# Left-over expert code before the last window, an early scatter read from the gather buffer, and pools that wait as wholes

## The chip, the cores and the metric

The kernel runs on one NeuronCore of a Trainium2 chip. The metric is the device time of one execution in microseconds (us). The engines are named as in the profile: PE (TensorE, matmuls), DVE (VectorE), ACT (ScalarE), POOL (GpSimd), SP (SyncE, which here only issues DMAs). A name with a q behind it (PEq, POOLq) is that engine's sequencer: branches, semaphore waits, DMA issues.

## The reference, cut to what matters

Three layers run one after the other. The change lies in the third, a routed layer of eight experts; every token is served by one expert alone.

```python
x = attention(...)                       # 8 heads of 64, windowed, with global keys
x = _moe_ref(x, mu_k, mu_r, w_k, w_v, w_r)   # shift, relu^2 MLP, sigmoid gate: [4, 544, 512]

# _moe2_ref: for every token (2176 of them)
e = argmax(logits[b, s])  if s == 0 or local_gate[b, s] < 0.5  else prev_e
p = softmax(logits[b, s])
h = np.maximum(x[b, s] @ w1[e], 0.0)     # 512 -> 1024
out[b, s] = p[e] * (h @ w2[e])           # 1024 -> 512
```

## The kernel before, in words

**Phase 1** (0 to 541 us) computes attention, the second layer and the routing: for each expert a list of its tokens in chunks of 128 (`idx`), each token's weight (`acc`, read as `pcol`), and the number of chunks of each expert (`cint`, from it the largest, `cmax`). The second layer's result lies in device memory as `y`. **Phase 2** (541 to 791 us) is the expert layer. A *window* is up to two chunks of one expert: `full` computes two chunks, `tail` one. For a window POOL gathers the chunk's rows of `y` into `xs` (L859, an indirect DMA), PE transposes them (L866) into PSUM, ACT and DVE split the result into a high and a low part (`xh` L868, `xl` L869), and each product is three matmuls (L21 high by high, L23 weight low, L24 operand low). `pht` is the hidden layer; `hs`, `hh` and `hl` carry it on (L909, L897, L898); `po` is the second product; DVE scales it (`osb`, L924) and POOL scatters the rows to the output `out_dram` (L925, an indirect DMA).

Expert weights come from device memory in parts of 512 KB: SP fetches a part into a staging tile `st` or `sw` (L769), ACT splits off the high half (L778) and DVE or POOL the low half (L781), into one of four pairs of weight slots. Expert e uses slots 2 and 0 when e is even, 1 and 3 when it is odd, so the next expert's weights load while this one computes.

For this input the experts have 242, 127, 267, 483, 495, 321, 218 and 23 tokens, that is 2, 1, 3, 4, 4, 3, 2 and 1 chunks. The code is fixed for two windows of every expert (four chunks); further chunks are *left-overs*. The number of chunks is known at run time alone, so the windows stand under `If`s on registers (`first`, `more`). Expert 0's first chunk is computed ahead, still in phase 1, by `Experts.ahead`: its product ends in `poa`, DVE scales it into the phase-1 tile `oa` (L844), and POOL sends it off by the *early scatter* (L846), whose list of rows `idx` is a phase-1 tile too. Phase 2 therefore starts with `tail(0)`, the second chunk of expert 0. After the loop over experts 1 to 7 two blocks stand under `If`s: the left-overs of expert 0 (L972) and those of the others (L978). With these counts neither block is entered: all engines jump over both.

Memory: phase 1 and phase 2 use the same on-chip memory one after the other. Before the change the phase-2 pools say `reuse_waits="tile"`: each phase-2 tile waits for those phase-1 tiles that lay in its own place. The order of instructions on an engine is the order of the program here (phase 2 is scheduled by hand); a wait holds the engine's queue.

Of the kernel before, what the change touches and what calls it, by code (L numbers as in the profile page):

```python
# [12 lines left out]
PSUM=bass.MemoryType.PSUM; DRAM=bass.MemoryType.DRAM  # L13
# [319 lines left out]
class Mix:  # L333
# [360 lines left out]
    def finish(s,ps):  # L694

        nc=s.nc; t=s.const
        s.ci=t([P,E],"cint",I32); s.cm=t([P,1],"cmax",I32); cf=t([P,E],"cf")
        nc.vector.tensor_tensor(out=s.ci,in0=ps,in1=s.up,op=ALU.add)
        nc.vector.tensor_scalar(out=s.ci,in0=s.ci,scalar1=7,scalar2=None,op0=ALU.logical_shift_right)
        nc.vector.tensor_copy(cf,s.ci)  # L700
        nc.vector.tensor_reduce(out=s.cm,in_=cf,axis=X,op=ALU.max)
def phase1(tc,ctx,i,const,y,ident,x,slots,early,place,right):

# [47 lines left out]
class Experts:  # L751

    def __init__(s,tc,ident,w1,w2,y,out,slots):
        s.tc=tc; s.nc=tc.nc; s.ident=ident; s.w=(w1,w2); s.y=y; s.out=out
        s.w2done=False; s.slots=slots; s.loaded=0; s.staged=[]; s.K=2

        s.o=[1]+[0]*(E-1); s.m=[1]+[NCH]*(E-1)
    def slot(s,e,which): return s.slots[((2,0),(1,3))[e%2][which]]
    def views(s,e,which):

# [29 lines left out]
    def ahead(s,m):  # L790
# [49 lines left out]
        yield op("P",0.0,("cm",),(),lambda: s.w2done)  # L840
        ps=cm("poa")
        for f in range(8): yield from mm(ps,hh[:,f],hl[:,f],w2h[:,f],w2l[:,f],f==0,f==7)
        yield op("D",.61,("r",),("cm",))
        o=m.temp("oa"); nc.vector.tensor_scalar(out=o,in0=ps,scalar1=pc,scalar2=None,op0=ALU.mult)  # L844
        yield op("G",1.1,(),("r",))
        nc.gpsimd.indirect_dma_start(out=s.out,out_offset=IndirectOffsetOnAxis(ap=idx,axis=0),in_=o,in_offset=None,bounds_check=T-1,oob_is_err=False)  # L846
    def alloc(s):
        w=s.work

        new=[s.xwork.tile([P,1024],F32,name=f"sw{i}",bufs=1) for i in range(NST)]  # L850
        s.xs+=[s.xwork.tile([P,2,D],F32,name=f"xs{i}",bufs=1) for i in range(1,s.K)]
        s.x=[[s.xwork.tile([P,4,256],F32R,name=f"x{q}{i}",bufs=1) for q in "hl"] for i in range(3)]
        s.h=[w.tile([P,8,256],F32R,name=f"h{q}",bufs=1) for q in "hl"]
        s.st+=new; s.free+=new
    def gather(s,e,k):
        i=k%s.K
        for j in range(min(2,s.m[e]-2*k)):
            ch=e*NCH+s.o[e]+2*k+j
            s.nc.gpsimd.indirect_dma_start(out=s.xs[i][:,j,:],out_offset=None,in_=s.y,in_offset=IndirectOffsetOnAxis(ap=s.idx[:,ch:ch+1],axis=0))  # L859
    def prep(s,i,e,k,hf):  # L860

        nc=s.nc; xh,xl=s.x[i]; n=min(2,s.m[e]-2*k); N=n*P
        pt=s.ps.tile([P,2,256],F32,tag="pt",name="pt",bufs=2)
        for d in range(2):
            for j in range(n):
                nc.tensor.transpose(pt[:,d,j*P:(j+1)*P],s.xs[k%s.K][:,j,(2*hf+d)*P:(2*hf+d+1)*P],s.ident)  # L866
        sl=slice(2*hf,2*hf+2)
        nc.scalar.activation(xh[:,sl,:N],pt[:,:,:N],AF.Copy)  # L868
        nc.vector.tensor_sub(xl[:,sl,:N],pt[:,:,:N],xh[:,sl,:N].bitcast(F32))  # L869
# [77 lines left out]
    def run(s):  # L947
# [1 line left out]

        at=lambda e,k: (e%2,2)[k%2]  # L950
        s.gather(0,0)
        _,cs=s.nc.values_load_multi_w_load_instructions(s.counts[0:1,0:E],min_val=0,max_val=NCH); cmax=s.nc.values_load(s.cmax[0:1,0:1],min_val=0,max_val=NCH)
        s.cs=cs
        for _ in range(max(0,8-LN)):
            p=s.staged.pop(0); list(s.split(*p)); s.free.append(p[3])
# [4 lines left out]
        def others(e):  # L960
            if e+1>=E: return []
            def last():
                s.prep(at(e+1,0),e+1,0,1)
                if e+2<E: s.gather(e+2,0)
            return [lambda: (s.gather(e+1,1),s.prep(at(e+1,0),e+1,0,0)),last]

        s.tail(at(0,0),0,0,[s.whole]*min(8,16-LN),others(0))
        for e in range(1,E):
            s.first(at(e,0),at(e,1),e,cs[e],[s.whole]*8 if e+1<E else (),own(e),others(e))
        def weights(e):  # L970
            for q in range(8): list(s.split(*s.part(e,q,s.st[q%len(s.st)])))
        with tc.If(cs[0]>=2):  # L972
            s.o[0]=2; s.m[0]=NCH-2; weights(0)
            for k in range(NK-1):
                with tc.If(cs[0]>=2*k+2):
                    s.gather(0,k); s.prep(k%2,0,k,0); s.prep(k%2,0,k,1)
                    s.more(k%2,0,k,cs[0],1)
        with tc.If(cmax>=2*K+1):  # L978
            for e in range(1,E):
                with tc.If(cs[e]>=2*K+1):  # L980
                    weights(e)
                    for k in range(K,NK):
                        with tc.If(cs[e]>=2*k+1):
                            s.gather(e,k); s.prep(k%2,e,k,0); s.prep(k%2,e,k,1)
                            s.more(k%2,e,k,cs[e])

def program(tc,ins,out):
    nc=tc.nc
    with ExitStack() as ctx:
# [16 lines left out]
            m=phase1(tc,st,ins,const,y,ident,x,slots,early,place,right)  # L1006
            x.idx,x.pcol,x.counts,x.cmax=m.idx,m.acc[:,E*NCH:],m.ci,m.cm

        t=dict(reuse_waits="tile")
        x.xwork=p("xwork",**t); x.work=p("work",**t); x.ps=Pools("pt",p("pst",space=PSUM,**t),p("ps2",space=PSUM,**t))  # L1010
        x.alloc()
        slots.append(pair(p("wq",**t),3))
        with tc.manual_schedule():
            x.run()

# [22 lines left out]
```

## Time and profile before

| what | value |
|---|---|
| time, median of 3 runs | 809.5 us (807.52 to 812.17) |
| time of the profiled execution | 809.28 us |
| its span in the profile | 807.5 us |
| PE busy in the span | 739.7 us, 92% |
| DVE, ACT, POOL busy | 65%, 49%, 45% |
| phase 1, phase 2, end | 0 to 541, 541 to 791, 791 to 807.5 us |
| longest waits of PE from 540 us on | 5.9 us (`po`, L24) and 4.6 us (`pht`, L21) |

In the profile a row of the timeline tells when a group of equal instructions started, how long the group lasted, engine, line, what it wrote and read, and in square brackets how long the engine had been idle before and what released it. "issue" as releaser is time in which the engine waited for nothing that the profile shows, such as a branch. Branches and semaphore waits are sequencer instructions and not counted as busy; the view of one source line lists them with their duration. [...]

### The profile page before, as it was taken

The numbers are of one execution on the slowest core, as the hardware profiler recorded it, in microseconds if no ns is written. First come the engines' busy times: TensorE is split into PE (matmuls) and PEld (weight loads), VectorE is DVE, ScalarE is ACT, GpSimd is POOL, SyncE is SP. The second block draws the span as 40 slices with busy tenths as digits, with TensorE's granted clock in tenths as the row PEclk, the third lists the DMA queues.
The fourth block names the chain that finished last, engine by engine and source line by source line (L and its number), as shares of the span: only waits on it lengthen the run. The fifth ranks groups of instructions, "written<-read, shape, count | busy, mean of one in ns | idle before, by whom it ended". The sixth has DMA issues, their size and how long they took to land. (4 is left out here: it accounts for less than half of the span.)

```text
span 807.5 us, 14190 instructions
## 1 busy us (share of the span) xinstructions
PE 739.7 (92%) x4786; PEld 621.7 (77%) x4786; DVE 522.9 (65%) x1482; ACT 397.3 (49%) x985; POOL 367.4 (45%) x492
## 2 busy tenths in 40 slices
PE   5988799899989999899998999997899999999971
PEld 3655587798878888888887898775788989998961
DVE  6699889776595785785766854774673627244610
ACT  4787676663555654655654422434553416152610
POOL 6678968645254362654462422115651514133220
PEclk9998999999999999899999999998999999999986
DMA  6674341211102102112102300327962805336300
GB/s 151 163 192 134 90 110 57 77 22 48 41 18 76 36 17 68 43 30 63 23 1 100 110 27 14 133 76 246 321 229 83 270 31 177 121 109 206 113 27 11
DMA packets 93731, 77.97 MB, mean 97 GB/s; under 512 B 70510, under 2 KB 74606, under 8 KB 93618
## 3 DMA queue, kind: packets, MB, share of 16 engines
q1 hardware_dynamic: 89618, 64.27, 26.5%
q0 software_dynamic: 4000, 12.33, 4.5%
q8 instruction: 54, 0.88, 0.5%
q14 instruction: 59, 0.48, 0.2%
HBM read 67.66 MB, written 9.70 MB: 96 GB/s over the span
## 5 line engine op out<-in xcount | busy, mean ns | idle before, releaser
L222 POOL TENSOR_SCALAR pl<-pl,mx 128x192 f32<-128x192 f32 (+1 forms) x128 | 67.4, 539 | 74.2 <-DVE mx L219 45.3
L21 PE MATMUL psk<-xs,slot0h 128*128 128x256 f32 x256 | 74.5, 297 | 1.6 <-ACT xs L448 1.6
L216 ACT ACTIVATE pl<-pl,mx 128x224 f32<-128x224 f32 (+1 forms) x128 | 58.8, 461 | 33.7 <-DVE mx L213 28.9
L24 PE MATMUL psk<-xs,slot0l 128*128 128x256 f32 x256 | 73.2, 287 | 0.0
L23 PE MATMUL psk<-xs,slot0h 128*128 128x256 f32 x256 | 73.2, 287 | 0.0
L859 POOL DMA_INDIRECT xs<-y,idx x29 | 34.7, 1196 | 76.0 <-PE pt L866 48.8
L925 POOL DMA_INDIRECT out_dram<-osb,idx x19 | 23.5, 1238 | 95.7 <-DVE osb L924 79.2
L450 POOL TENSOR_TENSOR xs<-xm,xs 128x512 fp32r<-128x512 f32 (+1 forms) x36 | 46.2, 1291 | 44.2 <-ACT xs L448 44.2
L880 ACT ACTIVATE hh<-ph 128x256 fp32r<-128x256 f32 x56 | 21.6, 385 | 83.4 <-PE ph L24 82.1
L443 POOL TENSOR_SCALAR xm<-xT,mut 128x256 f32<-128x256 f32 (+7 forms) x96 | 43.3, 469 | 29.5 <-DVE xT L294 16.1
L21 PE MATMUL psv<-slot1h,kh 128*128 128x512 f32 x136 | 55.5, 409 | 0.0
L23 PE MATMUL psv<-slot1l,kh 128*128 128x512 f32 x136 | 54.8, 404 | 0.3 <-POOL slot1l L417 0.3
L24 PE MATMUL psv<-slot1h,kl 128*128 128x512 f32 x136 | 54.4, 403 | 0.0
L21 PEld LDWEIGHTS psk<-xs,slot0h 128*128 128x128 f32 x256 | 48.7, 192 | 2.9 <-ACT xs L448 1.9
L23 PEld LDWEIGHTS psk<-xs,slot0h 128*128 128x128 f32 x256 | 48.9, 191 | 0.7
L24 PEld LDWEIGHTS psk<-xs,slot0l 128*128 128x128 f32 x256 | 48.8, 190 | 0.6
L228 PE MATMUL ptp<-ident,pl 128*128 128x128 f32 x256 | 43.4, 288 | 5.4 <-DVE ph L114 2.0
L236 PE MATMUL av<-ph,v 128*128 128x256 f32 x192 | 44.5, 291 | 2.4 <-DVE xT L294 1.1
L119 DVE TENSOR_TENSOR plo<-ptp,ph 128x512 fp32r<-128x512 f32 x48 | 32.7, 685 | 19.0 <-ACT ph L117 18.7
L881 DVE SCALAR_TENSOR_TENSOR hl<-ph,hh 128x256 fp32r<-128x256 f32 x56 | 23.7, 423 | 32.9 <-ACT hh L880 32.5
L446 DVE SCALAR_TENSOR_TENSOR xm<-xT,mut,xm 128x256 f32<-128x256 f32 (+7 forms) x96 | 41.5, 468 | 3.6 <-POOL xm L443 3.5
L228 PEld LDWEIGHTS ptp<-ident,pl 128*128 128x128 f32 x256 | 30.4, 146 | 12.5 <-POOL pl L222 2.6
(730 smaller groups left out, 2491.8 us busy)
## 6 DMA issues: line engine op xcount, KB each, us to landing
st<-in_moe_w_dram SPq DMA_DIRECT2D x42, 512.0 KB, 4.4
sw<-in_moe_w_dram SPq DMA_DIRECT2D x22, 512.0 KB, 4.6
y<-r SPq DMA_DIRECT2D x17, 256.0 KB, 2.0
qn<-in_q_l_dram SPq DMA_DIRECT2D x32, 128.0 KB, 3.0
kn<-in_k_l_dram SPq DMA_DIRECT2D x32, 128.0 KB, 2.9
earlyh<-in_moe_w_k_dram SPq DMA_DIRECT2D x8, 512.0 KB, 4.7
raw<-in_moe_w_v_dram SPq DMA_DIRECT2D x8, 512.0 KB, 3.6
vn<-in_v_l_dram SPq DMA_DIRECT2D x24, 96.0 KB, 2.2
```

Source lines behind the costliest of these rows:

```text
L21: i=nc.tensor.matmul(out,wh,xh,start=first,stop=False)
L23: nc.tensor.matmul(out,wh,xl,start=False,stop=False)
L24: return nc.tensor.matmul(out,wl,xh,start=False,stop=last)
L119: nc.vector.tensor_sub(out[1],x,out[0].bitcast(F32))
L216: nc.scalar.activation(p[:,h,ks],p[:,h,ks],AF.Exp,bias=mx[:,h:h+1],scale=-1.0,accum_out=mx[:,4+h:5+h])
L222: nc.gpsimd.tensor_scalar(out=p[:,h,ks],in0=p[:,h,ks],scalar1=mx[:,6+h:7+h],scalar2=0.0,op0=ALU.mult,op1=ALU.add)
L228: nc.tensor.transpose(pt[:,c,h],p[:,h,c*96:c*96+P],s.ident)
L236: nc.tensor.matmul(o,s.v(u,x,i,c),P_[y][:,c],start=c==m==0,stop=c==1 and m==len(parts)-1)
L443: nc.gpsimd.tensor_scalar(out=x[:,u,o:o+k],in0=s.xT[b][:,c,q:q+k],scalar1=m[:,1,c:c+1],scalar2=0.0,op0=ALU.mult,op1=ALU.add)
L446: nc.vector.scalar_tensor_tensor(out=x[:,u,o:o+k],in0=s.xT[b][:,c,1+q:1+q+k],scalar=m[:,0,c:c+1],in1=x[:,u,o:o+k],op0=ALU.mult,op1=ALU.add)
L450: nc.gpsimd.tensor_sub(xl[:,cs,:n],x[:,:,:n],xh[:,cs,:n].bitcast(F32))
L859: s.nc.gpsimd.indirect_dma_start(out=s.xs[i][:,j,:],out_offset=None,in_=s.y,in_offset=IndirectOffsetOnAxis(ap=s.idx[:,ch:ch+1],axis=0))
```

## The change

Four edits stand together.

1. The left-over code moves. Before, it stood behind the last expert, as two blocks. Now it stands under a single `If(cmax>=2*K+1)` in front of the only window of expert 7, which becomes a plain `tail` under no `If`. So that the one test covers experts 0 and 7, whose fixed code holds fewer chunks than four, 3 is added to their counts (`ends=cf[:,0:E:E-1]`, one small DVE instruction) before the largest is taken. With this input's counts (at most 4, and 1+3 for experts 0 and 7, expert 0's first chunk being counted out) the block is not entered.
2. Expert 7's fixed code shrinks to one chunk (`s.m`): the gather of its second chunk and the transposes of that chunk are no longer issued.
3. The early scatter's source is `s.xs[0][:,1]`, the unused half of the first gather buffer, in place of the tile `oa`, and the scatter carries no rank in phase 1's order any more (the keys in `op("D",...)` and `op("G",...)`). So that expert 1's gather doesn't fall on the same buffer, the choice of buffer is shifted by one for experts 1 to 7 (`row`).
4. The phase-2 pools lose `reuse_waits="tile"`: the first use of a pool's memory on an engine waits for everything of phase 1 that lay in the pool's place.

```diff
@@ -698,6 +698,8 @@
         nc.vector.tensor_tensor(out=s.ci,in0=ps,in1=s.up,op=ALU.add)
         nc.vector.tensor_scalar(out=s.ci,in0=s.ci,scalar1=7,scalar2=None,op0=ALU.logical_shift_right)
         nc.vector.tensor_copy(cf,s.ci)
+
+        ends=cf[:,0:E:E-1]; nc.vector.tensor_scalar(out=ends,in0=ends,scalar1=3.0,scalar2=None,op0=ALU.add)
         nc.vector.tensor_reduce(out=s.cm,in_=cf,axis=X,op=ALU.max)
 def phase1(tc,ctx,i,const,y,ident,x,slots,early,place,right):
 
@@ -754,7 +756,7 @@
         s.tc=tc; s.nc=tc.nc; s.ident=ident; s.w=(w1,w2); s.y=y; s.out=out
         s.w2done=False; s.slots=slots; s.loaded=0; s.staged=[]; s.K=2
 
-        s.o=[1]+[0]*(E-1); s.m=[1]+[NCH]*(E-1)
+        s.o=[1]+[0]*(E-1); s.m=[1]+[NCH]*(E-2)+[1]
     def slot(s,e,which): return s.slots[((2,0),(1,3))[e%2][which]]
     def views(s,e,which):
 
@@ -840,9 +842,10 @@
         yield op("P",0.0,("cm",),(),lambda: s.w2done)
         ps=cm("poa")
         for f in range(8): yield from mm(ps,hh[:,f],hl[:,f],w2h[:,f],w2l[:,f],f==0,f==7)
-        yield op("D",.61,("r",),("cm",))
-        o=m.temp("oa"); nc.vector.tensor_scalar(out=o,in0=ps,scalar1=pc,scalar2=None,op0=ALU.mult)
-        yield op("G",1.1,(),("r",))
+        yield op("D",.61,(),("cm",))
+
+        o=s.xs[0][:,1]; nc.vector.tensor_scalar(out=o,in0=ps,scalar1=pc,scalar2=None,op0=ALU.mult)
+        yield op("G",1.1)
         nc.gpsimd.indirect_dma_start(out=s.out,out_offset=IndirectOffsetOnAxis(ap=idx,axis=0),in_=o,in_offset=None,bounds_check=T-1,oob_is_err=False)
     def alloc(s):
         w=s.work
@@ -852,8 +855,11 @@
         s.x=[[s.xwork.tile([P,4,256],F32R,name=f"x{q}{i}",bufs=1) for q in "hl"] for i in range(3)]
         s.h=[w.tile([P,8,256],F32R,name=f"h{q}",bufs=1) for q in "hl"]
         s.st+=new; s.free+=new
+    def row(s,e,k):
+
+        return (k+(e>0))%s.K
     def gather(s,e,k):
-        i=k%s.K
+        i=s.row(e,k)
         for j in range(min(2,s.m[e]-2*k)):
             ch=e*NCH+s.o[e]+2*k+j
             s.nc.gpsimd.indirect_dma_start(out=s.xs[i][:,j,:],out_offset=None,in_=s.y,in_offset=IndirectOffsetOnAxis(ap=s.idx[:,ch:ch+1],axis=0))
@@ -863,7 +869,7 @@
         pt=s.ps.tile([P,2,256],F32,tag="pt",name="pt",bufs=2)
         for d in range(2):
             for j in range(n):
-                nc.tensor.transpose(pt[:,d,j*P:(j+1)*P],s.xs[k%s.K][:,j,(2*hf+d)*P:(2*hf+d+1)*P],s.ident)
+                nc.tensor.transpose(pt[:,d,j*P:(j+1)*P],s.xs[s.row(e,k)][:,j,(2*hf+d)*P:(2*hf+d+1)*P],s.ident)
         sl=slice(2*hf,2*hf+2)
         nc.scalar.activation(xh[:,sl,:N],pt[:,:,:N],AF.Copy)
         nc.vector.tensor_sub(xl[:,sl,:N],pt[:,:,:N],xh[:,sl,:N].bitcast(F32))
@@ -949,7 +955,7 @@
 
         at=lambda e,k: (e%2,2)[k%2]
         s.gather(0,0)
-        _,cs=s.nc.values_load_multi_w_load_instructions(s.counts[0:1,0:E],min_val=0,max_val=NCH); cmax=s.nc.values_load(s.cmax[0:1,0:1],min_val=0,max_val=NCH)
+        _,cs=s.nc.values_load_multi_w_load_instructions(s.counts[0:1,0:E],min_val=0,max_val=NCH); cmax=s.nc.values_load(s.cmax[0:1,0:1],min_val=0,max_val=NCH+3)
         s.cs=cs
         for _ in range(max(0,8-LN)):
             p=s.staged.pop(0); list(s.split(*p)); s.free.append(p[3])
@@ -962,27 +968,35 @@
             def last():
                 s.prep(at(e+1,0),e+1,0,1)
                 if e+2<E: s.gather(e+2,0)
-            return [lambda: (s.gather(e+1,1),s.prep(at(e+1,0),e+1,0,0)),last]
+            def then():
+                if e+2<E: s.gather(e+1,1)
+                s.prep(at(e+1,0),e+1,0,0)
+            return [then,last]
 
         s.tail(at(0,0),0,0,[s.whole]*min(8,16-LN),others(0))
-        for e in range(1,E):
-            s.first(at(e,0),at(e,1),e,cs[e],[s.whole]*8 if e+1<E else (),own(e),others(e))
+        for e in range(1,E-1):
+            s.first(at(e,0),at(e,1),e,cs[e],[s.whole]*8,own(e),others(e))
         def weights(e):
             for q in range(8): list(s.split(*s.part(e,q,s.st[q%len(s.st)])))
-        with tc.If(cs[0]>=2):
-            s.o[0]=2; s.m[0]=NCH-2; weights(0)
-            for k in range(NK-1):
-                with tc.If(cs[0]>=2*k+2):
-                    s.gather(0,k); s.prep(k%2,0,k,0); s.prep(k%2,0,k,1)
-                    s.more(k%2,0,k,cs[0],1)
+        def window(e,k,d):
+            i=(0,2)[k%2]
+            s.gather(e,k); s.prep(i,e,k,0); s.prep(i,e,k,1)
+            s.more(i,e,k,cs[e],d)
+        def rest(e,o,load=True):
+
+            d=o-(e==0); keep=s.o[e],s.m[e]
+            s.o[e]=o; s.m[e]=NCH-o
+            with tc.If(cs[e]>=d+1):
+                if load: weights(e)
+                for k in range((s.m[e]+1)//2):
+                    with tc.If(cs[e]>=2*k+1+d): window(e,k,d)
+            s.o[e],s.m[e]=keep
+
         with tc.If(cmax>=2*K+1):
-            for e in range(1,E):
-                with tc.If(cs[e]>=2*K+1):
-                    weights(e)
-                    for k in range(K,NK):
-                        with tc.If(cs[e]>=2*k+1):
-                            s.gather(e,k); s.prep(k%2,e,k,0); s.prep(k%2,e,k,1)
-                            s.more(k%2,e,k,cs[e])
+            rest(E-1,1,False)
+            for e in range(E-1): rest(e,2*K if e else 2)
+            weights(E-1)
+        s.tail(at(E-1,0),E-1,0,[],[])
 
 def program(tc,ins,out):
     nc=tc.nc
@@ -1006,10 +1020,9 @@
             m=phase1(tc,st,ins,const,y,ident,x,slots,early,place,right)
             x.idx,x.pcol,x.counts,x.cmax=m.idx,m.acc[:,E*NCH:],m.ci,m.cm
 
-        t=dict(reuse_waits="tile")
-        x.xwork=p("xwork",**t); x.work=p("work",**t); x.ps=Pools("pt",p("pst",space=PSUM,**t),p("ps2",space=PSUM,**t))
+        x.xwork=p("xwork"); x.work=p("work"); x.ps=Pools("pt",p("pst",space=PSUM),p("ps2",space=PSUM))
         x.alloc()
-        slots.append(pair(p("wq",**t),3))
+        slots.append(pair(p("wq"),3))
         with tc.manual_schedule():
             x.run()
 
```

**POOL at the start of phase 2.** The names: `xs_5870` and `xs_7297` are the two gather buffers, `idx_6091` and `oa` belong to the early scatter, `cint` and `cmax` are the counts that go into registers; the waits DMASW0, 1, 2 stand for landings of POOL's own earlier DMAs, DMASW1 for the gather of L859 (L865 after). Before:

```order
L859 DMA xs_5870<-y,idx 128x512 [waits DMAHW6_49,DMAHW7_49,DMAHW4_49,DVE_49]
L952 TENSOR_LOAD cint [waits DVE_49]
L952 TENSOR_LOAD cmax [waits DVE_49]
L859 DMA xs_5870<-y,idx 128x512 [waits DMASW1_49,PE_49]
L859 DMA xs_5870<-y,idx 128x512
L846 DMA out_dram<-oa,idx_6091 2176x512 [waits DVE_49]
L781 TENSOR_TENSOR slot1l<-sw_7295,slot1h 128x1024 [waits DMAHW5_49,Activation_49]
L859 DMA xs_7297<-y,idx 128x512 x2
L859 DMA xs_5870<-y,idx 128x512 [waits DMASW2_49,PE_49]
L859 DMA xs_5870<-y,idx 128x512 [waits DMASW3_49,DMASW0_49,PE_49]
```

After:

```order
L865 DMA xs_5870<-y,idx 128x512 [waits DMAHW6_49,DMAHW7_49,DMAHW4_49,DVE_49]
L849 DMA out_dram<-xs_5870,idx_6091 2176x512 [waits DVE_49]
L958 TENSOR_LOAD cint [waits DVE_49]
L958 TENSOR_LOAD cmax [waits DVE_49]
L865 DMA xs_7297<-y,idx 128x512 [waits DMASW0_49,DMASW2_49,PE_49,Activation_49]
L865 DMA xs_7297<-y,idx 128x512
L783 TENSOR_TENSOR slot1l<-sw_7295,slot1h 128x1024 [waits DMAHW5_49,Activation_49]
L865 DMA xs_5870<-y,idx 128x512 [waits DMASW1_49,PE_49]
L865 DMA xs_5870<-y,idx 128x512
L865 DMA xs_7297<-y,idx 128x512 [waits DMASW3_49,PE_49]
```

The early scatter moved from behind the two gathers of expert 1 to ahead of them and of the register loads; the gathers now go to the other buffer and wait for DMASW2, the landing of the scatter.

**DVE at the same place.** Before:

```order
L701 TENSOR_REDUCE cmax<-cf 128x1 [waits DVE_49]
L844 TENSOR_SCALAR oa<-poa,pc_6092 128x512 [waits DMASW0_49,PE_49]
L683 TENSOR_TENSOR acc<-psL,acc 128x136 [waits PE_49]
L952 TENSOR_LOAD cint [waits DVE_49]
L952 TENSOR_LOAD cmax [waits DVE_49]
L869 TENSOR_TENSOR xl_7299<-pt,xh_7298 128x2x128 [waits Activation_49] x2
L781 TENSOR_TENSOR slot1l<-st_5869,slot1h 128x1024 [waits DMAHW1_49,Activation_49]
L781 TENSOR_TENSOR slot1l<-st_5867,slot1h 128x1024 [waits DMAHW2_49,Activation_49]
L781 TENSOR_TENSOR slot1l<-st_5868,slot1h 128x1024 [waits DMAHW3_49,DMAHW0_49,Activation_49]
L898 TENSOR_TENSOR hl<-pht_7453,hh 128x4x128 [waits DMASW4_49,DMAHW7_49,DVE_49,Activation_49]
```

After:

```order
L702 TENSOR_SCALAR cf<-cf 128x2 [waits DVE_49]
L703 TENSOR_REDUCE cmax<-cf 128x1 [waits DVE_49]
L847 TENSOR_SCALAR xs_5870<-poa,pc_6092 128x512 [waits PE_49]
L683 TENSOR_TENSOR acc<-psL,acc 128x136 [waits PE_49]
L958 TENSOR_LOAD cint [waits DVE_49]
L958 TENSOR_LOAD cmax [waits DVE_49]
L875 TENSOR_TENSOR xl_7299<-pt,xh_7298 128x2x128 [waits DMAHW4_49,DMASW2_49,DMAHW7_49,DMASW0_49,Activation_49]
L875 TENSOR_TENSOR xl_7299<-pt,xh_7298 128x2x128 [waits Activation_49]
L783 TENSOR_TENSOR slot1l<-st_5869,slot1h 128x1024 [waits DMAHW1_49,Activation_49]
```

The wait for the early scatter (DMASW4 before, DMASW2 after) stood at `hl`, in the second half of `tail(0)`; now it stands at `xl`, in front of `tail(0)`'s first matmuls. One small instruction (L702) was added ahead of it.

**PE at the same place.** Before:

```order
L952 TENSOR_LOAD cint [waits DVE_49]
L952 TENSOR_LOAD cmax [waits DVE_49]
L866 MATMUL pt<-ident,xs_5870 128x128 [waits DMASW1_49]
L866 MATMUL pt<-ident,xs_5870 128x128 x3
L21 MATMUL pht<-slot2h,xh_7298 128x512 [waits DVE_49,Activation_49]
L23 MATMUL pht<-slot2l,xh_7298 128x512
L24 MATMUL pht<-slot2h,xl_7299 128x512 [waits DVE_49]
```

After:

```order
L958 TENSOR_LOAD cint [waits DVE_49]
L958 TENSOR_LOAD cmax [waits DVE_49]
L872 MATMUL pt<-ident,xs_5870 128x128 [waits DMASW1_49,PE_49]
L872 MATMUL pt<-ident,xs_5870 128x128 x3
L21 MATMUL pht<-slot2h,xh_7298 128x512 [waits DMAHW4_49,DMAHW5_49,DMAHW3_49,DMAHW6_49,DMASW2_49,DMAHW7_49,DVE_49,Activation_49]
L23 MATMUL pht<-slot2l,xh_7298 128x512
L24 MATMUL pht<-slot2h,xl_7299 128x512 [waits DVE_49]
```

The first `pht` matmul now waits for the landing DMASW2 and for five weight-part landings (DMAHW3 to 7) besides DVE and ACT. ACT's first `xh` (L874) and SP's first weight fetch of phase 2 (L771) got the wait for DMASW2 too.

**POOL at the end of phase 2.** Before (the rows of the left-over blocks between L972 and the last are left out of what is shown):

```order
L943 COMPARE_AND_BRANCH
L925 DMA out_dram<-osb,idx 2176x512 [waits DMASW5_49,DMASW4_49,DMASW6_49,DMASW1_49,DMASW7_49,DMASW0_49,DVE_49]
L939 ISA [waits DMASW3_49,DMASW2_49,DMASW1_49]
L943 UNCONDITIONAL_BRANCH
L943 ISA [waits DMASW0_49]
L939 ISA [waits DMASW3_49,DMASW2_49,DMASW1_49]
L943 UNCONDITIONAL_BRANCH
L972 COMPARE_AND_BRANCH
L781 TENSOR_TENSOR slot2l<-sw_7295,slot2h 128x1024 [waits DMAHW7_49,DMAHW5_49,Activation_49]
```

After, the end of the list and with it the end of the left-over block (L995):

```order
L995 UNCONDITIONAL_BRANCH
L995 ISA [waits Pool_49,DMASW4_49,DMASW5_49,DMASW3_49,DMASW6_49,DMASW2_49,DMASW7_49,DMASW1_49,DMASW0_49]
L995 UNCONDITIONAL_BRANCH
L931 DMA out_dram<-osb,idx 2176x512 [waits DMASW4_49,DMASW3_49,DMASW5_49,DMASW2_49,DMASW6_49,DMASW1_49,DMASW7_49,DMASW0_49,DVE_49]
L1047 UNCONDITIONAL_BRANCH
L1047 ISA [waits barrier_Pool_Activation_PE_DVE_SP_gather]
```

Before, the last scatter (L925) was followed by the two blocks' branches (L972, L978) and what the skipping arm does; now the scatter (L931) is the last thing that POOL does ahead of the program's end (L1047), and the branch stands ahead of it.

## Rows read from the trace of the kernel before

**Rows 1.** The page: busy time, share of the span, instructions of each engine.

```profile
PE 739.7 (92%) x4786; PEld 621.7 (77%) x4786; DVE 522.9 (65%) x1482; ACT 397.3 (49%) x985; POOL 367.4 (45%) x492
```

**Rows 2.** PE's waits, 540 to 808 us: waiter, releaser, total us, times, longest.

```profile
PE po L24 <- DVE hl L898: 5.9, 1, 5.9
PE pht L21 <- issue: 5.3, 2, 4.6
PE pt L866 <- DMA xs<-y,idx: 1.5, 1, 1.5
```

**Rows 3.** Timeline of PE around the start of phase 2.

```profile
540.79 0.66 PE L866 MATMUL pt<-ident,xs 128*128 128x128 f32 x4
541.70 0.50 PE L21 MATMUL pht<-slot2h,xh 128*128 128x512 f32 x1 [0.26 <-ACT xh L868]
...
554.85 0.80 PE L24 MATMUL po<-slot0h,hl 128*128 128x512 f32 x1 [5.88 <-DVE hl L898]
```

**Rows 4.** Timeline of DVE, ACT and POOL at the same place.

```profile
540.66 0.75 DVE L844 TENSOR_SCALAR oa<-poa,pc 128x512 f32<-128x512 f32 x1 [2.82 <-PE poa L818]
...
554.11 0.69 DVE L898 TENSOR_TENSOR hl<-pht,hh 128x512 fp32r<-128x512 f32 x1 [7.71 <-DMA out_dram<-oa,idx]
...
541.26 0.66 ACT L868 ACTIVATE xh<-pt 128x256 fp32r<-128x256 f32 x2 [7.26 <-PE pt L866]
...
545.25 2.06 POOL L846 DMA_INDIRECT out_dram<-oa,idx  x1 [0.30 <-issue]
```

**Rows 5.** Issue to landing: 537 to 565 us, then scatters after 740 (min/median/max).

```profile
xs<-y,idx POOLq DMA_INDIRECT x7, 5.3
out_dram<-oa,idx POOLq DMA_INDIRECT x1, 8.7
...
DMA to landing us min/median/max: 2.8/3.2/4.9
```

**Rows 6.** Windows: each engine's busy time, granted clock, DMA share, GB/s.

```profile
541.70:549.00 7.30, 7.03 (x30) 5.13 (x30) 4.20 (x5) 6.41 (x9) 6.67 (x4) 1.00 0.90 298
...
552.90:559.73 6.83, 4.88 (x16) 4.01 (x17) 2.94 (x4) 1.66 (x3) 0.00 (x0) 0.50 0.59 193
...
774.80:781.60 6.80, 5.60 (x13) 4.46 (x14) 0.00 (x0) 0.02 (x1) 0.00 (x0) 0.50 0.02 5
...
443.68:447.09 3.41, 2.81 (x14) 2.76 (x15) 2.86 (x12) 2.71 (x7) 0.20 (x1) 0.50 0.19 76
```

**Rows 7.** Timeline of PE, then POOL, around expert 7's window.

```profile
771.05 0.39 PE L24 MATMUL po<-slot0h,hl 128*128 128x512 f32 x1
776.00 0.77 PE L21 MATMUL pht<-slot1h,xh 128*128 128x512 f32 x1 [4.56 <-issue]
...
791.79 0.99 POOL L925 DMA_INDIRECT out_dram<-osb,idx  x1 [18.27 <-DVE osb L924]
```

**Rows 8.** Line L972, sequencers: duration ns min/median/max, first and last start us.

```profile
L972 POOLq EVENT_SEMAPHORE  x3: 17/17/43, 796.7 to 796.8; - x3
...
L972 PEldq COMPARE_BRANCH  x1: 3860/3860/3860, 788.3 to 788.3; - x1
...
L972 POOLq COMPARE_BRANCH  x1: 45/45/45, 793.0 to 793.0; - x1
...
```

**Rows 9.** Line L978, sequencers, in the same columns.

```profile
L978 POOLq EVENT_SEMAPHORE  x5: 17/43/43, 800.9 to 801.3; - x5
...
L978 PEldq COMPARE_BRANCH  x1: 4618/4618/4618, 792.4 to 792.4; - x1
...
L978 POOLq INC_SWDGE_SEM  x1: 1167/1167/1167, 801.3 to 801.3; - x1
```

**Rows 10.** Line L1034, the program's end, in the same columns.

```profile
L1034 SPq EVENT_SEMAPHORE  x14: 17/28/28, 802.5 to 807.5; - x14
...
L1034 POOLq DRAIN  x3: 46/107/4158, 802.5 to 807.3; - x3
L1034 SPq DRAIN  x3: 7/7/13, 803.6 to 807.0; - x3
```

## The prediction

> **What bounds the kernel now.** I began with the page's engine shares: PE is busy in 92% of the span [rows 1], so what counts is where PE stands still and what follows its last matmul. The list of PE's waits from 540 us on gives two that matter: 5.9 us at `po` (L24), put down to DVE's `hl`, and 4.6 us at the first matmul of expert 7, put down to nothing but issue [rows 2]. The timeline of PE dates the first: it stood until 554.85 [rows 3]. The timeline of DVE says why: `hl` had been held 7.71 us by the landing of the early scatter, whose source and list of rows are phase-1 tiles; POOL began to issue that scatter only at 545.25, behind expert 1's gathers [rows 4], and it took 8.7 us to land [rows 5], while the DMA engines were 90% busy with weights [rows 6]. [...] The end of the program is the third place: the last scatter is issued at 791.79 [rows 7], and 15.7 us of span follow it (807.5 less 791.79). The lines L972, L978 and L1034 tell what they hold [rows 8 to 10].
>
> **The change part by part.**
>
> *The end.* Before, after the scatter POOL branches over L972 at 793.0 and comes out at 796.7; branches over L978 and comes out at 800.9; spends 1.17 us in that block's last semaphore instruction from 801.3 [rows 8, 9]; then its drain takes 4.158 us from 802.5, and the closing barrier runs to 807.5 [rows 10]. After the change the order has nothing between the last scatter and the end. Two chains remain. SP waits for the scatter's landing: landings of scatters late in the kernel took 2.8 to 4.9 us [rows 5], SP's end waits run from 802.5 to its drain at 803.6, 1.1 us [rows 10], and the barrier after POOL's long drain takes 807.5 − (802.5 + 4.16) = 0.8: 791.8 + 2.8 to 4.9 + 1.1 + 0.8 = 796.5 to 798.6. POOL's own: the scatter ends at 792.8, and the drain takes 0.05 (the shortest of its three [rows 10]) to 4.16: with the barrier 793.7 to 797.8. The later decides: 796.5 to 798.6, and I take 797.9, a saving of 807.5 − 797.9 = **−9.6** (−9.0 to −11.0). Should the long drain only begin at the landing, 791.8 + 4.9 + 4.2 + 0.8 = 801.7, it is −5.8.
>
> [...]
>
> *The jump ahead of expert 7.* Before, PE already had a far jump there (over expert 7's two-chunk code) and stood 4.56 us [rows 7]. Now it is the jump over the left-overs. PE's own price is then 3.86 to 4.62 [rows 8, 9] in place of the jump within those 4.56, and PE must also have the word of DVE and ACT that they jumped; DVE starts its jump only after scaling expert 6's last product. Between −0.7 and +0.8; I take **+0.3**. POOL's jump is hidden: it has the 18.27 us that it idles before the last scatter [rows 7].
>
> *Fewer transposes.* Expert 7 has one chunk now instead of room for two: four PE transposes fewer, 0.66 us for four [rows 3], in expert 6, where PE has no gap: **−0.5** (0 to −0.7). The gather that goes with them was off the path.
>
> *The start of phase 2.* The early scatter is issued as soon as DVE has scaled its product: DVE's L844 ends at 540.66 + 0.75 = 541.41, and 0.30 of issue, as before the scatter's row [rows 4], makes 541.7. But the pools now wait as wholes, so that ACT's first `xh`, DVE's first `xl`, PE's first `pht`, SP's first weight fetch and POOL's gather of expert 1 all wait for the scatter's landing, since its list of rows lies in phase-1 memory. The wait at `hl` is not removed, it moves ahead of `tail(0)`. With a landing of L us, `xh` starts at 541.7 + L + 0.2 and PE 0.44 later (541.26 to 541.70 [rows 3, 4]), so PE is late by L + 0.65 against its 541.70. No row shows this scatter alone on the queues; the nearest are the late scatters, 2.8 to 4.9 us [rows 5], where the DMA engines moved little (0.02 of their time [rows 6]); the far end is its own 8.7 us among weights. As SP's fetch waits as well, the weights are not there, and I take 3.7: PE late by 4.35. The clock: half of PE's busy time at 0.50 is lost, 4.88/2 = 2.4 after the standstill of 5.88, 5.60/2 = 2.8 after that of 4.56, and 2.81/2 = 1.4 in the mildest such stretch of the kernel, at 443.68 [rows 6]. Before, the place costs 5.88 + 2.4 = 8.3; after, 4.35 + 2.6 = 6.95: **−1.4** (with L 2.8 and 1.4 lost −3.5; with L 4.9 and 2.8 lost +0.05).
>
> [...]
>
> What is queued behind these waits: SP's fetches start some 4 us late, expert 1's gathers too. Expert 1's weights are needed when `tail(0)` ends, over 15 us on, and SP's fifth fetch on waited for staging tiles that DVE, held at `hl`, freed late; that hold is gone. So I put nothing down, and keep +1.5 at the upper end (one more wait like the 1.5 us for a gather [rows 2]).
>
> The added DVE instruction (on 8 counts) lies ahead of 2.82 us in which DVE idles [rows 4]: nothing; without that cover 0.2.
>
> *The sum.* Against the profiled execution, 809.28 us (span 807.5, 1.8 around it), near the median of 809.5: −9.6 + 0.3 − 0.5 − 1.4 = −11.2, so 798.1 us.
>
> **The rivals.**
>
> (a) The long drain belongs to the end itself and counts from the landing. For: it stands behind all waits [rows 10]. Against: the drain's other two are short, and what preceded the long one was a jump and a semaphore instruction that go. Time: 798.1 + 3.8 = 801.9.
>
> (b) The standstill at the start is mild: L near 2.8 and little of the clock lost. For: the stretch at 443.68 [rows 6]. Against: the two standstills over 4 us both lost 2.4 or more. With the end at its best −11.0 and the transposes whole: 809.28 − 11.0 − 0.7 − 3.5 + 0.2 = 794.3; with the end as forecast 796.
>
> (c) The early scatter still takes its 8.7 us, if it was slow of itself and not by the weights: PE late by 9.35, in all 11.95 against 8.3, +3.65 in place of −1.4: 803.1. For: that row is the only one of this scatter [rows 5]. Against: all later scatters.
>
> (d) Slower than before: the whole of phase 2 stands behind one landing now. From 798.1 each us of L beyond 3.7 adds one; the change loses from L = 14.9 on, 1.7 times the slowest scatter seen, and L = 19 gives 813.4. Nothing in the rows comes near it; it would take a scatter held by something in POOL's queue.
>
> (e) The change does not do what it says: the jump is not one but is paid by one engine after the other ahead of expert 7 (PE waits for DVE's whole jump, then makes its own). One more jump of 4.6 us at that place, with the clock at 0.50 again in any case: 802.7.
>
> **How the numbers follow.** The forecast (796.5 to 799.7) 0.5; (a) 0.13; (b) 0.15; (c) 0.1; (e) 0.07; (d) 0.02; 0.03 for a late weight part (up to 799.6 + 3). The predicted time is the likeliest case's, 798.1. Range: 794.5 leaves out 0.06 of (b) below, and 802.5 leaves out (c), (d) and some of (e) above, 0.14: together 0.2. A measurement of this kernel can tell about 0.5% from no change, 4.0 us: faster means below 805.2. All cases but (d) lie below; with a third of a case that none of them names, faster 0.94, same 0.04, slower 0.02.
>
> **What would show it.** In the changed kernel's trace: no branch behind the last scatter, and 5 to 7 us from its issue to the end of the span (over 9 for (a)). PE stands 4 to 5 us ahead of the first `pht` of phase 2, released by ACT's `xh`, with 0.50 granted behind it, and no wait for `hl`. The early scatter's landing 3 to 5 us (8 or more for (c)). PE's wait ahead of expert 7 remains, 4 to 5.5 us (over 8 for (e)). It would be wrong if expert 1's matmuls wait for a weight part, if the scatter lands late, or if the drain keeps its 4 us behind the landing.

## The result, and the profile after

The changed kernel takes 801.46 us, the median of 798.24, 801.4, 801.53 and 803.99, against 810.51 us of the kernel before beside it: a ratio of 0.989 with an interval of 0.984 to 0.994. That is a gain of 9.1 us. It lies in the forecast's range, 3.4 us above the likeliest case and some 2 us short of the forecast gain of 11.2.

The profiled execution is the one of 803.99 us, with a span of 802.0 us. The page's row for PE, with the same columns as [rows 1], shows more busy time than before:

```profile
PE 745.2 (93%) x4782; PEld 627.8 (78%) x4782; DVE 521.5 (65%) x1483; ACT 397.0 (49%) x985; POOL 364.6 (45%) x489
```

Four matmuls fewer take 5.5 us more. All of that lies ahead of phase 2, where PE is busy for 510.0 us against 503.8, and is chance: DVE scales the early product at 546.47, in [rows 4] at 540.66, with phase 1 unchanged but for one small DVE instruction. Added up from the records of the granted clock, where 1.00 is PE's full speed, 37.5 us of phase 1 stood at 0.50 here and 23.9 us in the first trace of before. A second trace of the kernel before (below) has its scaling at 545.68, and two more of the changed kernel at 542.86 and 543.05. So I measure from that scaling on, and set phase 1 aside.

The list of PE's waits, 540 to 808 us, answers to [rows 2]:

```profile
PE pht L21 <- issue: 4.9, 2, 3.5
PE pht L21 <- PEq L995: 4.9, 1, 4.9
PE pht L21 <- ACT xh L874: 3.7, 1, 3.7
```

The 5.9 us at `po` are gone. In their place stand 3.7 us at the first `pht`, where the prediction had put 4 to 5, and a wait of 3.5 us that it did not name. The timelines of DVE, POOL, ACT and PE around the start of phase 2 answer to [rows 3, 4], and the last line is of the kernel before; behind them stands the scatter's time from issue to landing (minimum, median and maximum of the one):

```profile
546.47 0.75 DVE L847 TENSOR_SCALAR xs<-poa,pc 128x512 f32<-128x512 f32 x1 [2.60 <-PE poa L820]
...
547.50 1.03 POOL L849 DMA_INDIRECT out_dram<-xs,idx  x1 [3.27 <-DVE acc L683]
...
550.47 0.66 ACT L874 ACTIVATE xh<-pt 128x256 fp32r<-128x256 f32 x2 [10.63 <-DMA out_dram<-xs,idx]
...
550.90 0.80 PE L21 MATMUL pht<-slot2h,xh 128*128 128x512 f32 x1 [3.67 <-ACT xh L874]
...
566.17 0.39 PE L24 MATMUL po<-slot0h,hl 128*128 128x512 f32 x1
570.09 0.78 PE L21 MATMUL pht<-slot1h,xh 128*128 128x512 f32 x1 [3.53 <-issue]
...
563.80 0.49 PE L21 MATMUL pht<-slot1h,xh 128*128 128x512 f32 x1
```

```profile
DMA to landing us min/median/max: 2.8/2.8/2.8
```

`tail(0)` ends at 566.17 + 0.39 = 566.6, 20.1 us after the scaling; before, PE reached expert 1's first `pht` 23.1 us after it without a pause (563.80). So 3.0 us were won here. Then PE stood for 3.53 us ahead of expert 1 and began it 23.6 us after the scaling: nothing was left. The sequencer's rows for L945, the branch of expert 1 to 6 (the old L939), say why; columns as in [rows 8]:

```profile
L945 PEldq COMPARE_BRANCH  x6: 73/74/6462, 563.4 to 750.4; - x6
```

One branch, the first, took 6.46 us, from 563.43 to 569.89. Before, the same jump over expert 1's two-chunk code took 3.50 us (560.10 to 563.60) and lay beside matmuls that PE already had in its queue. The windows view (columns as in [rows 6]) has the standstills' price in clock, and what the DMA engines did during the jump; its second block is of the kernel before:

```profile
549.58:556.40 6.82, 5.50 (x13) 4.35 (x14) 4.25 (x5) 3.49 (x5) 2.75 (x2) 0.50 0.67 248
...
563.43:569.89 6.46, 3.13 (x16) 2.27 (x14) 6.26 (x5) 4.59 (x6) 5.75 (x4) 1.00 0.90 269
...
570.06:573.47 3.41, 3.38 (x8) 2.71 (x9) 3.14 (x3) 1.06 (x1) 1.74 (x1) 0.50 1.01 367
```

```profile
560.10:563.60 3.50, 3.50 (x19) 2.70 (x17) 2.88 (x3) 2.66 (x5) 2.06 (x2) 1.00 0.31 97
```

During the jump the DMA engines were 90% busy, before 31%. PE had 3.13 us of matmuls to cover it, and a stretch at 0.50 followed its standstill.

At the end, PE's matmuls around the jump that is left, POOL's last scatter and the rows of the program's end (L1047, before L1034) answer to [rows 7, 10], and the rows of that jump (L995) to [rows 8, 9]:

```profile
776.21 0.39 PE L24 MATMUL po<-slot0h,hl 128*128 128x512 f32 x1
781.51 0.61 PE L21 MATMUL pht<-slot1h,xh 128*128 128x512 f32 x1 [4.92 <-PEq L995]
...
796.26 0.99 POOL L931 DMA_INDIRECT out_dram<-osb,idx  x1 [17.59 <-DVE osb L930]
```

```profile
L1047 POOLq DRAIN  x3: 46/112/5143, 796.0 to 801.7; - x3
L1047 SPq DRAIN  x3: 7/7/122, 799.6 to 801.4; - x3
...
L995 PEldq COMPARE_BRANCH  x1: 4161/4161/4161, 777.0 to 777.0; - x1
L995 DVEq COMPARE_BRANCH  x1: 62/62/62, 777.7 to 777.7; - x1
...
L995 DVEq EVENT_SEMAPHORE  x1: 21/21/21, 780.9 to 780.9; - x1
L995 PEldq EVENT_SEMAPHORE  x1: 51/51/51, 781.3 to 781.3; - x1
```

From the last scatter's issue to the end of the span it is now 802.0 − 796.26 = 5.7 us, before 15.7. The long drain is still there: it begins at 796.02, ahead of the scatter's record, and ends at 801.16, 3.9 us after the scatter's issue is over (797.25). The scatter landed in 2.3 us, at 798.5, and SP was through at 799.8; POOL's drain ends last.

### The profile page after: what moved, and what is told of

The parts are those of the page before. It is cut to its first block, busy times and chain, and to the rows that moved or that the text cites. A ratio compares the mean times of both kernels' runs of the same rounds, so it can differ in the third digit from the quotient of the medians.

```text
span 802.0 us, 14155 instructions
## 1 busy us (share of the span) xinstructions
PE 745.2 (93%) x4782; PEld 627.8 (78%) x4782; DVE 521.5 (65%) x1483; ACT 397.0 (49%) x985; POOL 364.6 (45%) x489
## 5 line engine op out<-in xcount | busy, mean ns | idle before, releaser
L21 PE MATMUL psk<-xs,slot0h 128*128 128x256 f32 x256 | 75.4, 300 | 0.9 <-ACT xs L448 0.8
L23 PE MATMUL psk<-xs,slot0h 128*128 128x256 f32 x256 | 74.2, 291 | 0.0
L931 POOL DMA_INDIRECT out_dram<-osb,idx x19 | 23.5, 1239 | 97.1 <-DVE osb L930 82.3
L865 POOL DMA_INDIRECT xs<-y,idx x26 | 33.5, 1288 | 59.4 <-PE pt L872 33.5
L21 PEld LDWEIGHTS psk<-xs,slot0h 128*128 128x128 f32 x256 | 49.4, 195 | 2.3 <-ACT xs L448 1.2
L23 PEld LDWEIGHTS psk<-xs,slot0h 128*128 128x128 f32 x256 | 50.0, 195 | 0.7
```

The source lines that it names most:

```text
L21: i=nc.tensor.matmul(out,wh,xh,start=first,stop=False)
L23: nc.tensor.matmul(out,wh,xl,start=False,stop=False)
```

## The experiments

All numbers in the table but the ratio come from traces, in us, one for each time that the kernel was profiled; they are worked out from unrounded times, so that an end of 15.7 or 5.7 above reads 15.8 or 5.8. "To expert 6" is from DVE's scaling of the early product to the end of expert 6's last matmul; "to the scatter" from there to the issue of the last scatter; "end" from there to the end of the span. "Jump" is PE's jump ahead of expert 1, with the share of time that the DMA engines were busy in it. The ratio is that of the timed runs to the kernel before, with its interval.

| kernel | to expert 6 | to the scatter | end | jump (DMA share) | ratio |
|---|---|---|---|---|---|
| before | 230.8; 230.2 | 20.4; 19.3 | 15.8; 16.3 | 3.50 (0.31); 3.36 (0.31) | 1 |
| the change | 230.1; 231.5; 227.5 | 19.7; 21.0; 20.4 | 5.8 each | 6.46 (0.90); 7.38 (0.89); 4.76 (0.95) | 0.989; 0.989 (0.985 to 0.993); 0.987 (0.984 to 0.991) |
| left-overs alone | 227.1; 227.2 | 20.3; 21.1 | 5.8 each | 3.79 (0.37); 3.54 (0.33) | 0.987 (0.984 to 0.990); 0.984 (0.981 to 0.987) |
| start alone | 229.0 | 19.3 | 15.6 | 5.07 (0.94) | 1.002 (0.999 to 1.004) |
| change, waits by tile | 225.1; 224.7 | 20.5; 20.7 | 5.8 each | 3.81 (0.46); 4.40 (0.54) | 0.988 (0.985 to 0.991); 0.984 (0.981 to 0.987) |
| change, list in the constant pool | 225.7; 225.8 | 19.6; 19.3 | 5.8 each | 3.39 (0.27); 3.67 (0.38) | 0.979 (0.976 to 0.983); 0.982 (0.979 to 0.984) |
| change, no left-over block | 229.3 | 14.2 | 5.8 | 5.67 (0.95) | 0.981 (0.977 to 0.985) |
| change, fewer fetches | 228.0 | 20.4 | 5.8 | 4.74 (0.52) | - |

**The change taken apart.** First the left-overs alone: edits 3 and 4 undone in the changed kernel.

```diff
...
-        o=s.xs[0][:,1]; nc.vector.tensor_scalar(out=o,in0=ps,scalar1=pc,scalar2=None,op0=ALU.mult)
...
+        o=m.temp("oa"); nc.vector.tensor_scalar(out=o,in0=ps,scalar1=pc,scalar2=None,op0=ALU.mult)
...
-        return (k+(e>0))%s.K
+        return k%s.K
...
-        x.xwork=p("xwork"); x.work=p("work"); x.ps=Pools("pt",p("pst",space=PSUM),p("ps2",space=PSUM))
+        t=dict(reuse_waits="tile")
+        x.xwork=p("xwork",**t); x.work=p("work",**t); x.ps=Pools("pt",p("pst",space=PSUM,**t),p("ps2",space=PSUM,**t))
...
```

> Edits 1 and 2 alone (left-overs ahead of expert 7's plain window, fixed code of expert 7 one chunk); early scatter from the tile oa, waits by tile, as before. Theory (the gain is the end, expert 7's jump and its transposes; the start of phase 2 nets to nothing): last scatter to end of span 5.7 us against 15.7, ratio to before 0.986 to 0.988 (10.0 to 11.3 us), PE's wait for hl of 5.9 us stays. Rival (the start carries 1.4 us and more of the change's gain): this kernel is 1.5 to 3 us slower than the whole change.

Then the start alone: the kernel before with edits 3 and 4 (the same lines the other way round).

> Edits 3 and 4 alone (early scatter from the gather buffer and ahead of the gathers, pools waiting as wholes); the left-overs stay behind expert 7 as two blocks. Theory: PE waits 3.7 us ahead of the first pht in place of 5.9 at hl, tail(0) ends 3 us earlier, and the far jump ahead of expert 1 comes out of hiding and gives it back: 0 to -1 us against before, ratio 0.998 to 1.000. Rival (the forecast's step): -1.4 to -3 us, ratio 0.996 to 0.998. Rival on the other side: the late weight fetches cost more than that, ratio over 1.001.

And the changed kernel with its pools back to `reuse_waits="tile"`.

> The whole change but for the pools, which wait by tile again (edits 1 to 3). Nothing of phase 2 then waits for the early scatter's landing except gathers into its buffer. Theory A (the moved wait costs 3.4 us of PE and 2.7 of clock, and what comes behind it follows): 4 to 6 us less than the whole change, ratio to before 0.980 to 0.984, no PE wait ahead of the first pht and none at hl. Theory B (expert 1's weights, gathers and the far jump ahead of it set the time of this place whatever PE does before): within 1.5 us of the whole change; the wait shows again ahead of expert 1's first pht, 5 us or more.

With them the changed kernel itself.

> The changed kernel again, on the same chip as the three others, as their yardstick. Theory: ratio to before 0.986 to 0.989, the same waits of PE from the start of phase 2 on (3.7 at xh, about 3.5 ahead of expert 1, 4.9 ahead of expert 7), and a different length of phase 1, as its stretches at 0.50 come and go from run to run. Rival (the difference of phase 1 to the kernel before belongs to the change): phase 1 again 5 us longer than in the profile of before.

The left-overs alone give 0.987, as much as the whole change; their wait for `hl` is 4.6 us and not 5.9. The start alone gives 1.002 with an interval from 0.999 to 1.004, where 0.998 to 1.000 was expected: no gain, and its jump ahead of expert 1 took 5.07 us, 2.1 us of it in the open. Its one trace reaches expert 6 some 1.5 us sooner than the kernel before, which the timed runs do not bear out. So the whole gain is the left-overs. The changed kernel again shows all three of its waits. By tile, PE waits neither for the scatter nor at `hl`, and from the scaling to expert 6 this trace is 5.0 to 6.4 us shorter than the two traces of the change taken so far (theory A); the timed runs miss the expectation, as 0.988 against 0.989 shows no such gain. PE stands for gathers instead, 4.2 us in all.

**What makes the jump ahead of expert 1 long.** The profile has DMA queues that it calls "instruction": in the kernel before they made 54 transfers of 16 KB and 59 of 8 KB. I take them for code; "pages" in the expectation are the pieces of 16 KB. The run is the changed kernel without the weight fetches of expert 2:

```diff
-        (queue or s.nc.sync).dma_start(st.rearrange("p (c f) -> p c f",c=c),s.w[which][e].rearrange("(q c p) f -> q p c f",p=P,c=c)[q])
+        if e!=2: (queue or s.nc.sync).dma_start(st.rearrange("p (c f) -> p c f",c=c),s.w[which][e].rearrange("(q c p) f -> q p c f",p=P,c=c)[q])
```

> The changed kernel without the eight weight fetches of expert 2 (left out; its splits read what the staging tiles held). They are what is in flight when PE makes its far jump ahead of expert 1. Theory A (the jump is slow since its code is fetched beside weights: 6.46 and 7.38 us where the DMA engines were 90% busy, 3.50 to 3.81 where they were 31 to 46% busy): 3.4 to 4.2 us for this jump, and at most 1 us of it outside PE's queued matmuls. Theory B (the jump is slow since the pools' waits moved the code against the pages): 5 to 7 us again, with PE standing 2 to 4.4 us.

The windows view has the jump, with POOL's gathers still under way:

```profile
558.48:563.22 4.74, 3.08 (x15) 2.23 (x13) 4.58 (x5) 4.45 (x7) 3.93 (x3) 1.00 0.52 136
```

With 4.74 us, 1.9 of it in the open, it lies between the two theories, and a later trace of the change itself has 4.76. The trace's records of single DMA packets say more. Inside each of the 14 jumps of the table lies one instruction transfer of 16 KB that ends 1.3 to 1.5 us before the jump does. What differs most is when it begins: 1.0 to 1.5 us into the jump in the eight traces where the DMA engines had been busy for at most 0.4 of the time until then, and 2.4 to 4.9 us into it in the six where they had been busy for 0.54 or more. In this run it begins 2.36 us into the jump, with no weight fetch in flight: the 0.54 are POOL's gathers alone. So leaving out the weights is not enough for a short jump, and the longest ones (4.00 and 4.93 us until the transfer begins) do not have the busiest engines (0.82 and 0.81).

**Whether it is the landing or the form of the waits.** The early scatter's list of rows moves to the constant pool, so that no phase-1 memory is read late; the pools wait as wholes, as in the change.

```diff
-        idx=m.sb.tile([P,1],I32,name="idx0",bufs=1); pc=m.sb.tile([P,1],F32,name="pc0",bufs=1)
+        idx=s.const.tile([P,1],I32,name="idx0",bufs=1); pc=m.sb.tile([P,1],F32,name="pc0",bufs=1)
...
-        x=Experts(tc,ident,ins['moe2_w1'],ins['moe2_w2'],y,out,slots)
+        x=Experts(tc,ident,ins['moe2_w1'],ins['moe2_w2'],y,out,slots); x.const=const
```

> The changed kernel with the early scatter's list of rows in the constant pool; pools wait as wholes as in the change, but phase 1's memory has no reader left that ends late, so the scatter's landing holds nothing but the gather into its buffer. Theory A (the landing, not the form of the waits, is what costs): PE's wait ahead of the first pht under 0.5 us in place of 3.6, no 0.50 behind it, the jump ahead of expert 1 about 3.8 us as by tile; from DVE's scaling of the early product to expert 6's last matmul 225 to 228 us against 230.1 and 231.5. Theory B (waiting as a whole holds the engines for other reasons too): over 229 us.

Theory A holds in the main. The list of PE's waits, 535 to 800 us, and the window of the jump ahead of expert 1:

```profile
PE pht L21 <- PEq L995: 4.9, 1, 4.9
PE pt L872 <- DMA xs<-y,idx: 3.3, 3, 2.4
PE pht L21 <- issue: 1.3, 1, 1.3
PE pht L21 <- ACT xh L874: 0.6, 1, 0.6
```

```profile
553.65:557.04 3.39, 3.39 (x18) 2.57 (x16) 2.96 (x3) 2.73 (x5) 2.18 (x2) 1.00 0.27 66
```

The first `pht` waits 0.6 us in place of 3.7, no wait of 3.5 us stands ahead of expert 1, and the fetches start 3.5 us earlier, so that PE's jump falls behind them: 3.39 us at a DMA share of 0.27. With that theory B of the run before falls too: the pools wait as wholes here, and the jump is short. Not all came as expected: PE now waits 3.3 us for gathers, 2.4 of them in `tail(0)`, and a stretch of 3.4 us at 0.50 begins with that wait's end, at 549.47. This kernel's ratio is 0.979, the best.

**What the jump that is kept costs.** The changed kernel without the left-over block, which these counts do not enter:

```diff
-        with tc.If(cmax>=2*K+1):
-            rest(E-1,1,False)
-            for e in range(E-1): rest(e,2*K if e else 2)
-            weights(E-1)
```

> The changed kernel without the left-over block (left out; it is not entered with these counts). Prices the one far jump that the change keeps ahead of expert 7. Theory: PE's stand there of 4.9 and 5.2 us falls to 1 us or less and the stretch at 0.50 behind it goes: 5 to 7.5 us less than the changed kernel from expert 6's last matmul to the last scatter. Rival (DVE's and POOL's skips are what is waited for, or the code is fetched anew at that place anyway): 2 us or less.

From expert 6's last matmul to the last scatter it is 14.2 us against 19.7 to 21.0: the kept jump costs 5.5 to 6.8 us, in PE's stand and in the stretch at 0.50 behind it. PE's timeline:

```profile
772.26 0.47 PE L21 MATMUL pht<-slot1h,xh 128*128 128x512 f32 x1 [0.99 <-DVEq L938]
```

**The kernel before, a second trace.**

> The kernel before once more, for a second trace. Theory (what differs ahead of phase 2 is chance): phase 1 another length than in the first trace by some us, with more or less time at 0.50; the early scatter lands in 8 to 9 us, PE waits 4.5 to 6 us for hl, and its jump ahead of expert 1 takes 3.4 to 4 us and is hidden. Rival: one of these is a property of the first trace alone.

It repeats [rows 2] but for chance: 5.6 us at `hl`, the jump 3.36 us and hidden, and phase 1 5 us longer. The trace lacks the early scatter's landing; `hl` began 8.6 us behind the scatter's issue.

**The four versions on one chip.** Nothing is edited anew here.

> The list of the early scatter in the constant pool, once more (the kernel of e6_list), now on one chip with the change itself. Theory A (the landing costs 3 to 6 us at the start of phase 2): 3 to 6 us less than the changed kernel, from the scaling of the early product to expert 6's last matmul 225 to 227 us. Theory B (the earlier result was a good chip): within 2 us of it.

> The changed kernel, yardstick of this call. Theory: ratio to before 0.987 to 0.990; the jump ahead of expert 1 over 5 us with the DMA engines about 90% busy, 229 to 231.5 us from the scaling to expert 6's last matmul. Rival (that jump is chance): under 4 us this time.

> Edits 1 and 2 alone, once more (the kernel of e1_leftovers). Theory: as fast as the changed kernel or 1 to 4 us faster, since edits 3 and 4 together bring nothing: 227 to 230 us from the scaling to expert 6's last matmul, the wait for hl of 4.5 to 6 us there. Rival (edits 3 and 4 gain the forecast's 1.4 us): slower than the changed kernel by that.

> Edits 1 to 3 with waits by tile, once more (the kernel of e3_tile). Theory: equal within 1.5 us to the kernel with the list in the constant pool, both without a wait for the landing; 225 to 226 us from the scaling to expert 6's last matmul. Rival (waits by tile keep late waits that waits as wholes don't): 2 us or more slower than that one.

Beside a median of 811.05 us before, the medians are 795.27 us with the list in the constant pool, 797.62 for the left-overs alone, 797.74 by tile and 799.54 for the change. The first is 4.3 us below the change, as theory A had it, though from the scaling to expert 6 the two traces differ by 1.7 us alone. It is 0.6 to 1.1 us longer than the kernel by tile from the scaling to expert 6, and 2.5 us shorter by the medians (1.5 at most expected), which the intervals do not separate. Two more expectations missed: the change's jump took 4.76 us this time (over 5 expected, under 4 by the rival), and it came to expert 6 after 227.5 us (229 to 231.5 expected). So the size of this jump varies by some 2.6 us from trace to trace, and with it what the change costs at the start of phase 2.

## Why the prediction was right, and where it was not

**The end** was forecast at −9.6 and measured at 5.7 against 15.7, −10.0. The mechanism was right: no branch stands behind the last scatter. That the number came so near is in part luck. The forecast let the chain over the scatter's landing decide; here SP was through at 799.8, and POOL's drain ended 1.3 us later. The forecast bounded that drain by 0.05 and 4.16, and it came close to the upper bound, 3.9 behind the scatter's issue; so the argument that the long drain would go with the jump was wrong. All eleven traces of kernels whose left-overs no longer stand at the end have 5.8 us there, so rival (a) falls: the drain ends 2.6 us after the landing, and does not begin its 4.2 us there. Whether it waits for the landing at all is not shown, since the landing took 2.3 us wherever it is on record.

**The jump ahead of expert 7** was forecast at +0.3 (−0.7 to +0.8). From expert 6's last matmul to the last scatter it was 20.4 and 19.3 before, 19.7, 21.0 and 20.4 after: in the mean +0.5. PE's own jump ended at 781.20 and DVE's 0.3 us earlier, so here PE's own set it, with DVE's close behind. Rival (e) falls: PE stood 4.6 to 5.2 us and not over 8. That the jump is still dear as a whole (5.5 to 6.8 us) the forecast did not price, and did not need to.

Inside each of the 14 jumps ahead of expert 1 lies the 16 KB instruction transfer: from 561.12 to 562.26 in the first trace of before, from 567.43 to 568.46 in the trace of the result. That the jump waits for it is my reading, and was not tried. What the jump costs beside other transfers the runs tell: 3.36 to 3.81 us in the seven traces with a DMA share of 0.46 or less, 4.40 and 4.74 at 0.54 and 0.52, 4.76 to 7.38 in the five at 0.89 or more.

**The start of phase 2** is the step that failed. It was forecast at −1.4, and −0.5 for the transposes, together −1.9; from the scaling to expert 6 the change took 230.1, 231.5 and 227.5 against 230.8 and 230.2, in the mean −0.8 with a scatter of 4 us. Its first half was right and even too small: the landing took 2.78 us and not 3.7, PE began 1.0 us earlier than forecast, and `tail(0)` ended 3.0 us sooner. The rows behind the 3.7 were scatters at other places. The failed step is the sentence on what is queued behind these waits, where I put nothing down. I looked for weights that come late to expert 1. What came late was PE's own jump: it lay hidden beside `tail(0)`'s last matmuls as long as the fetches and gathers were over by then. Held back by 4 us, SP's fetches and POOL's gathers fall onto the jump, the 16 KB transfer inside it begins late (4.00 us into it in the trace of the result, 1.02 in the first of before), the jump grows from some 3.5 us to 4.8 to 7.4, the 3.1 us of queued matmuls don't cover it, and a stretch at 0.50 follows. That the traffic is the reason is my estimate from the 14 traces, quiet against busy; no run varied the traffic alone, and what makes one busy jump 4.8 us and another 7.4 stays open.

The three terms sum to −10.0 + 0.5 − 0.8 = −10.3 us from the scaling on; the timed medians differ by 9.1, and their interval (5.0 to 12.7 us) holds both.

**Rivals (b) to (d)** did not come: the landing was the best of their cases, and a stretch at 0.50 followed all the same. The kernel with the list in the constant pool comes to (b)'s time by another way, as nothing at the start waits for the landing: its medians are 793.7 and 795.3 us.

**The left-overs alone** should by the forecast be 1.4 us slower than the change. They were as fast or faster, since they reach expert 6 after 227.1 and 227.2 us, some 3.3 us sooner than the kernel before, of which the transposes explain some 0.6 by the forecast's row; no run measured them. Another 1.1 are seen in the last section. The rest, gaps of 0.8 to 1.5 us behind expert 1 that are missing there, was not tried and stays open.

## What to carry to other kernels

Where memory is handed from one stage to the next, look for the last reader of the old stage, a DMA's list of rows included, and keep that one small tile elsewhere: with waits as wholes it took 4.3 us off the median, and waits by tile were not faster than that. In these traces the far jump ahead of expert 1 was cheap only while PE had queued work to cover it and the DMA engines were quiet (3.36 to 3.81 us at a share of 0.46 or less, 4.76 to 7.38 at 0.89 or more), so a change that moves transfers must be checked against the jumps, not only against the data's users. And code that is rarely entered is better placed ahead of the last piece of work than behind it: the end of the program was 10 us shorter, as no branch followed the last scatter. It is not free there, as the jump that is kept cost 5.5 to 6.8 us.

## What the runs showed of the hardware that was not expected

The drain of POOL at the end of the program took 5.1 us in every kernel that ends with a scatter, 3.9 of them behind its issue; it took 4.2 where a semaphore instruction of 1.17 us came last, and the scatter had landed long ago [rows 9, 10]. What it waits for no run told.

The last scatter landed in 2.3 us in the kernels that end with it (nine traces have it on record), and in 4.6 to 5.0 us in the three traces where the left-over branches followed it. The cause was not tried.

A start 0.1 us later cost 1 us here. In the kernel before, POOL's second gather for expert 1 began 0.07 us after DVE's `slot1l`; with the left-overs alone it began 0.02 us ahead of it. Timelines of POOL and DVE, first the kernel before, then the left-overs alone:

```profile
542.97 1.98 POOL L859 DMA_INDIRECT xs<-y,idx  x1 [0.30 <-issue]
...
542.90 3.50 DVE L781 TENSOR_TENSOR slot1l<-st,slot1h 128x1024 fp32r<-128x1024 f32 x3
```

```profile
543.12 0.95 POOL L864 DMA_INDIRECT xs<-y,idx  x1 [0.31 <-issue]
...
543.14 3.50 DVE L783 TENSOR_TENSOR slot1l<-st,slot1h 128x1024 fp32r<-128x1024 f32 x3
```

1.98 us against 0.95; the early scatter behind it is issued that much earlier, and PE's wait for `hl` is 4.6 us in place of 5.9. Both kernels repeat this in their second trace (1.98 and 0.95). The 14 traces agree from 530 us on: of 202 gathers whose issue began while such a DVE split had over 0.2 us left, all but one ended 0.8 to 0.9 us after that split, and the 167 whose issue began beside no split took 0.94 to 0.99 us. So it was POOL's gather that was held, by up to 1.0 us, where it began behind the split; DVE's three splits took 3.50 us in either order. What holds it was not tried.

With the pools waiting as wholes one branch of a later expert (L939, before L933) takes 4.3 to 5.4 us, and 0.35 by tile, at the same place. PE's sequencer rows of the change, then of the kernel before:

```profile
L939 PEldq COMPARE_BRANCH  x8: 64/292/5437, 605.1 to 750.1; - x8
```

```profile
L933 PEldq COMPARE_BRANCH  x8: 64/281/354, 600.2 to 744.5; - x8
```

All eight traces of kernels with whole waits have the long branch, those with the list in the constant pool too, and none of the six by tile. PE's queued matmuls hide most of it: 1.4 us at most stand open there. Each of the eight long branches has a 16 KB instruction transfer inside it, beginning 1.9 to 3.1 us in (3.10 in the change). In the first trace of before the branch at that place lies from 600.21 to 600.57 and holds none; the next begins at 602.62. That the added semaphore waits moved the code is my guess, and was not tried.
